# Attention and routed experts on one core: who rounds the keys and queries, how early inputs are fetched, and where the rank products stand

## The chip, the cores and the metric

The kernel runs on one core of a Trainium2 chip. The time is the device time of one launch in microseconds (us); three runs of the kernel before gave 1008.96, 1013.74 and 1014.48, the median is 1013.74. The engines named below are PE (TensorE, matrix products), ACT (ScalarE, activation functions and copies), DVE (VectorE), POOL (GpSimd, which also starts DMAs) and SP (SyncE, which starts most DMAs). Each works through a queue of its own in order, and waits at an instruction until what that needs has been signalled.

## What is computed

```python
# q, k, v: 8 batches x 12 heads x 448 tokens x 64, float32
scores = cap * tanh((q @ k^T / 8) / cap)             # cap = 30
attn   = softmax(scores);  x = attn @ v              # rows of 768 for 3584 tokens
logits = x @ w_gate + modality_bias[modality_id]     # 8 experts
e      = argmax(logits);  gate = softmax(logits)[e]
out    = gate * (relu(x @ w1[e]) @ w2[e])            # 768 -> 1024 -> 768, token's own expert only
```

## The kernel before

Attention works on 48 pairs of heads, `g` = 0 to 47 (six pairs to a batch); an iteration `g` of the loop in `attention` has four steps. The host lays keys (transposed, 512 columns) and queries (448 columns) of a pair side by side in one 128 x 960 tile `kq`. Products in full precision are made of three products of rounded numbers: `hi` is `kq` rounded, `lo` = `kq` - `hi`, and a score is hi·hi + lo·hi + hi·lo (L451). In steps 0 and 2 PE makes the scores of two steps, ACT takes tanh into `th` and exp into `pt` (three tiles) and `sh` (the last 64 keys of both heads). The weighting by values runs one pair behind: in step 1 `weigh_own` (L460) and in step 3 `weigh_shared` (L465) sum into one PSUM tile `xT`, which DVE copies out (L569). That PSUM tile has one buffer, so the next `weigh_own` waits for the copy. DVE also adds the exponentials up in two instructions, `tot` (L548, L549).

Three pairs make a group, and from the fourth pair on each pair also has a share of the work for the group before it. Call them the first, second and third pair (r = 0, 1, 2). The first and second pair's step 1 holds twelve products for sums and logits each (`sums`, L475, PSUM tile `glog`). The second pair's step 3 turns these to token order (`by_token`, tile `lt`) and computes `logits`. The third pair's step 3 is `rows_out`: three sets of four transpositions (L503) into PSUM tiles `tp`, each read by one DVE product into `xs` (L504), which POOL stores. The first and third set share one PSUM buffer, so PE's third set waits for DVE's first `xs`; the second set shares its buffer (tag `small`) with `rank`.

Every sixth pair a batch is complete. `route` then runs a chain of some 15 small DVE instructions to `oh` and `before`, yields, and is taken up again in step 1 of the next pair (a third pair): two small PE products into `rank` (L238, L240), small DVE instructions from there to `pos`, and four POOL DMAs that scatter into `mapd` (L264).

Who makes `hi`: for the first two pairs ACT and DVE; from then on POOL starts a second DMA of `kq` that writes the rounding tile (L436). It may start when PE has read the buffer's old contents; `hi` and `lo` have two buffers. It stands in POOL's queue with the scatters and stores. `prep(g + 1)`, called in step 1 of pair `g`, requests `kq` and `va` (values) over SP's queue; `kq` has two buffers, `va` three.

What sets the order: PE's instructions keep the order of the code (`pin`), and so do SP's loads. DVE's, ACT's and POOL's are put in order by a scheduler when the program is built, which may move an instruction before others of its engine.

At the end, after pair 45, `early_slot` chooses the first expert's rows. SP requests its weights `raw` (four at once), ACT and DVE split them between the last pairs (`SPLITS`, L672 and L673), POOL reads the map (`mt`, L649) and gathers the rows (`xg`, L656), and PE transposes these from step 3 of pair 47 on (`MOVES`, L692). From then on come the expert slots, which the change doesn't touch.

Of the kernel before, what the change touches and what calls it, by code (L numbers as in the profile page):

```python
# [39 lines left out]
F32 = mybir.dt.float32  # L40
# [9 lines left out]
B, H, S, D = 8, 12, 448, 64  # L50
C, CP = 4, 112
NP = H // 2
# [7 lines left out]
VW = 2 * KU * D + 128  # L60
# [15 lines left out]
class Program:  # L76
# [336 lines left out]
    def attention(self, qk, first, rp):  # L413
        tc, nc = self.tc, self.nc
        pe, pin = nc.tensor, self.pin
        with ExitStack() as st:
            ld = st.enter_context(tc.tile_pool(name="ld", bufs=3))
            sp = st.enter_context(tc.tile_pool(name="sp", bufs=2))
            pp = st.enter_context(tc.tile_pool(name="pp", bufs=2))
# [3 lines left out]
            ps_g = st.enter_context(tc.tile_pool(name="ps_g", bufs=1, space=PSUM))  # L423
            ps_v = st.enter_context(tc.tile_pool(name="ps_v", bufs=1, space=PSUM))

            def prep(g):
                b, hp = divmod(g, NP)
                kq = first if g == 0 else self.load_kq(qk, g)
                va = ld.tile([128, VW], F32, name="va")
                self.load(va, self.v[b, hp])  # L430
                hi = sp.tile([128, QK], F32R, name="hi")
                lo = sp.tile([128, QK], F32R, name="lo")
                keep = pin if g < 2 else (lambda inst: inst)

                if g > 1:
                    nc.gpsimd.dma_start(hi, self.kq[b, hp])  # L436
                for cs in (slice(0, QK),) if g else (slice(0, KC2), slice(KC2, QK)):
                    if g < 2:
                        keep((nc.scalar.copy if cs.start else nc.vector.tensor_copy)(hi[:, cs], kq[:, cs]))
                    keep(nc.vector.tensor_tensor(lo[:, cs], kq[:, cs], hi[:, cs], op=ALU.subtract))  # L440
                return hi, lo, va

# [68 lines left out]
            def store(h, xs):  # L511
# [3 lines left out]
                    xs,  # L515
                )

            NG = NP * B

            SPLITS = {  # L520
                (NG - 2, 1): (0,),
                (NG - 2, 3): (1,),
                (NG - 1, 1): (2,),
                (NG - 1, 3): (3,),
                (NG - 0, 0): (4,),
                (NG - 0, 1): (5,),
            }
            MOVES = {(NG - 1, 3): (0, 1), (NG, 1): (2, 3), (NG, 3): (4, 5)}
            self.warm(self.ps_r, 4)
            ready = prep(0)  # L530
            self.gate_weights()
            kept, lgs, routing, raws = {}, {}, {}, []
            for g in range(NG + 1):
                if g < NG:
                    pt = pp.tile([128, 2 * KU, S], F32, name="pt")
                    sh = xp.tile([128, S], F32, name="sh", bufs=HB + 2)
                    cur = ready
                for step in range(C):
                    if step % 2 == 0 and g < NG:
                        scores(step, pt, sh, *cur[:2])  # L540
                        scores(step + 1, pt, sh, *cur[:2])
                    if step == 1:
                        if g + 1 < NG:
                            ready = prep(g + 1)
                        if g:
                            ppt, psh, pva = pend
                            tot = xp.tile([128, 2, S], F32, name="tot", bufs=HB + 1)
                            nc.vector.tensor_tensor(tot, ppt[:, 0:2], ppt[:, 2:4], op=ALU.add)  # L548
                            nc.vector.tensor_tensor(tot, tot, ppt[:, 4:6], op=ALU.add)  # L549
                            xT = ps_x.tile([128, 512], F32, name="xT")  # L550
                            weigh_own(xT, ppt, pva)

                        if g > HB:
                            h, r = divmod(g - HB - 1, HB)
                            if r < 2:
                                sums(h, 2 * r)
                                sums(h, 2 * r + 1)
                        if g in routing:
                            next(routing[g], None)
                            del routing[g]  # L560
                    if step == 3:
                        if g == 3:
                            self.empty_map()
                        if g == 2:
                            self.gate_bias()
                        if g:
                            weigh_shared(xT, psh, pva)
                            xs_ = xp.tile([128, S], F32, name="xT", bufs=HB + 3)
                            nc.vector.tensor_copy(xs_, xT[:, :S])  # L569
                            kept[g - 1] = xs_, tot, psh  # L570
                        if g > HB:
                            h, r = divmod(g - HB - 1, HB)
                            b = h // NH
                            if r == 1:
                                if h % NH == 0:
                                    lgs[b] = xp.tile([CP, C, H, E], F32, name="lg")
                                lt = by_token()
                                rec = logits(h, lt, lgs[b])
                                if h % NH == NH - 1:
                                    way = self.route(b, lgs[b], rp, self.ps_r)  # L580
                                    next(way)
                                    routing[g + 1] = way
                            if r == 2:
                                xs = xp.tile([CP, C, HB * 128], F32, name="xs")
                                for t in range(HB):
                                    rows_out(h, t, xs, rec)
                                store(h, xs)
                                if h == NH * (B - 1) - 1:
                                    meta = self.early_slot(self.cpool, self.ps_r)
                    for k in SPLITS.get((g, step), ()):  # L590
                        self.split_w(raws[k], self.w1s[k], pin=True)
                        if len(raws) < KC:
                            raws.append(self.load_raw(e, self.w1, len(raws), FF))
                    for k in MOVES.get((g, step), ()):
                        self.transpose(k, (ps_s, self.ps_r)[k % 2], ("sc", "small")[k % 2], busy=k < 2)
                if g < NG:
                    pend = pt, sh, cur[2]
                if g == NG - 3:
                    e = self.expert(meta, 0)
                    early = e, self.rows(meta, 0)  # L600
                    raws = [self.load_raw(e, self.w1, k, FF) for k in range(self.nstage)]
                if g == NG - 2:
                    self.gather(early[1], known=NT - S)
# [328 lines left out]
    def build(self):  # L932
        tc, nc = self.tc, self.nc
        with ExitStack() as st:
            self.nstage = 4
            self.cpool = st.enter_context(tc.tile_pool(name="cpool", bufs=1))
            dram = st.enter_context(tc.tile_pool(name="dram", bufs=1, space=DRAM))
            self.plani = self.cpool.tile([1, 3], I32, name="plani")
            with ExitStack() as sa:
                qk = sa.enter_context(tc.tile_pool(name="qk", bufs=2))  # L940
                first = self.load_kq(qk, 0, parts=2)
                with tc.tile_pool(name="ps_w", bufs=1, space=PSUM) as ps_w:
                    self.constants(self.cpool, dram)
                    self.warm(ps_w, 6)
                big = nc.values_load(self.flag[0:1, 0:1], min_val=0, max_val=1)
                with tc.If(big == 0) as branch:
                    with ExitStack() as sb:
                        self.moe_pools(sb)
                        nc.gpsimd.memset(self.xg.bitcast(F32), 0.0)
                        self.ps_r = sb.enter_context(tc.tile_pool(name="ps_r", bufs=1, space=PSUM))  # L950
                        rt = sb.enter_context(tc.tile_pool(name="rt", bufs=1))
                        early, way = self.attention(qk, first, rt)
                        self.moe_pools2(sb)

                        def order():
                            self.meta = self.slots(rt, self.ps_r, True)

                        self.run_slots(early, ((1, lambda: next(way, None)), (3, order)))
                with branch.Else():
                    self.general()  # L960
                    self.tail(fresh=True)
# [70 lines left out]
```

## Time and profile before

| | |
|---|---|
| runs | 1008.96, 1013.74, 1014.48 us |
| profiled execution, its own time | 1010.09 us |
| its span | 1008.5 us |
| PE busy | 926.6 us, 92% |
| ACT busy | 557.2 us, 55% |
| DVE busy | 516.7 us, 51% |
| POOL busy | 157.9 us, 16% |
| granted TensorE clock, mean | 0.965 |
| DMA | 162.63 MB, 161 GB/s |

A group of instructions stands with its busy time, and with the idle time of its engine in front of it and what ended that. PE is busy nearly everywhere from 540 us on, in the expert slots. In the attention part it is busy some 90% of the time: what matters there is which wait ends last in front of PE, and whether the clock is full afterwards.

### The profile page before, as it was taken

Reading aid. Unit: us, or ns where it says so; the run is one execution under the profiler, and the core shown is the slowest. Engines: PE = TensorE matmul, PEld = TensorE weight load, DVE = VectorE, ACT = ScalarE, POOL = GpSimd, SP = SyncE. Lnnn points to the kernel's source line nnn. Section 1 sums busy time; section 2 is a strip of 40 time slices with the busy share of each in tenths; the row PEclk is TensorE's granted clock in tenths of the full one; section 3 lists DMA queues with packets and bytes.
Section 4 is the critical chain, followed back from the end, with each engine's and each line's share of the span. In section 5 each row is a group of like instructions: output and inputs, shape, how many; then the busy total and the mean of one; then the engine's idle time right before and its main releaser. Section 6 shows DMA issues by size and latency. Waiting matters only on the chain. (4 is left out here: it accounts for less than half of the span.)

```text
span 1008.5 us, 14612 instructions
## 1 busy us (share of the span) xinstructions
PE 926.6 (92%) x5360; PEld 709.5 (70%) x5360; DVE 516.7 (51%) x894; ACT 557.2 (55%) x759; POOL 157.9 (16%) x191
## 2 busy tenths in 40 slices
PE   8998998989897998948889999999999999999986
PEld 3444444444454444415889999999999999998886
DVE  4565565646455556727634444443434343428751
ACT  6986777768686778743344444444344344335541
POOL 2003021120212021220242020202020202020000
PEclk9999999999999999969999999999999999999997
DMA  4655646565455546383376363635453635347550
GB/s 137 186 179 120 200 114 193 148 155 177 130 192 126 178 111 215 105 242 98 90 252 225 120 224 121 216 128 190 130 210 129 203 129 190 108 132 259 204 177 5
DMA packets 53803, 162.63 MB, mean 161 GB/s; under 512 B 9422, under 2 KB 9934, under 8 KB 53712
## 3 DMA queue, kind: packets, MB, share of 16 engines
q1 hardware_dynamic: 38000, 105.78, 32.4%
q0 software_dynamic: 15568, 55.72, 19.4%
q8 instruction: 47, 0.77, 0.3%
q14 instruction: 44, 0.36, 0.1%
q10 hardware_dynamic: 144, 0.00, 0.0%
HBM read 139.96 MB, written 22.69 MB: 161 GB/s over the span
## 5 line engine op out<-in xcount | busy, mean ns | idle before, releaser
L453 ACT ACTIVATE th<-sc,isc 128x896 f32<-128x896 f32 x192 | 167.9, 908 | 110.9 <-PE sc L451 110.7
L723 PE MATMUL ph<-x,al 128*128 128x384 f32 (+2 forms) x528 | 168.0, 318 | 0.0
L748 PE MATMUL py<-bh,hh 128*128 128x384 f32 x464 | 159.4, 344 | 3.7 <-ACT hh L729 3.2
L748 PE MATMUL py<-bh,hl 128*128 128x384 f32 x464 | 155.8, 336 | 0.0
L748 PE MATMUL py<-bl,hh 128*128 128x384 f32 x464 | 155.7, 336 | 0.0
L455 ACT ACTIVATE pt<-th,cabs 128x896 f32<-128x896 f32 x144 | 148.0, 1042 | 2.0
L719 PE MATMUL ph<-x,ah 128*128 128x384 f32 x384 | 129.8, 338 | 1.0 <-DVE hl L730 1.0
L460 PE MATMUL xT<-pt,va 128*64 128x448 f32 x576 | 127.8, 582 | 1.9 <-DVE xT L569 1.9
L720 PE MATMUL ph<-x,ah 128*128 128x384 f32 x384 | 129.0, 336 | 0.0
L673 DVE TENSOR_TENSOR bl<-raw,bh 128x768 fp32r<-128x768 f32 x88 | 81.3, 954 | 57.4 <-ACT bh L672 57.1
L440 DVE TENSOR_TENSOR lo<-kq,hi 128x960 fp32r<-128x960 f32 (+2 forms) x49 | 55.6, 1137 | 105.6 <-DMA hi<-in_kq_dram 83.8
L451 PE MATMUL sc<-hi 64*128 64x448 f32 (+1 forms) x336 | 88.4, 453 | 21.5 <-DMA hi<-in_kq_dram 12.9
L672 ACT CAST bh<-raw 128x768 fp32r<-128x768 f32 x88 | 70.2, 839 | 65.3 <-DMA raw<-in_w_dram 57.0
L723 PEld LDWEIGHTS ph<-x,al 128*128 128x128 f32 x528 | 102.7, 194 | 0.0
L451 PEld LDWEIGHTS sc<-hi 64*128 64x128 f32 (+1 forms) x336 | 37.2, 190 | 88.6 <-issue 31.6
L673 DVE TENSOR_TENSOR al<-raw,ah 128x1024 fp32r<-128x1024 f32 x66 | 78.9, 1222 | 32.5 <-ACT ah L672 31.9
L758 POOL DMA_INDIRECT out_dram<-ot,mt x29 | 32.2, 1109 | 388.2 <-ACT ot L753 307.6
L748 PEld LDWEIGHTS py<-bh,hh 128*128 128x128 f32 x464 | 87.4, 188 | 4.8 <-ACT hh L729 3.9
L753 ACT ACTIVATE ot<-py,mt 128x384 f32<-128x384 f32 x58 | 33.6, 580 | 98.4 <-PE py L748 53.9
L460 PEld LDWEIGHTS xT<-pt,va 128*64 128x64 f32 x576 | 39.5, 146 | 68.7 <-issue 54.2
L748 PEld LDWEIGHTS py<-bl,hh 128*128 128x128 f32 x464 | 87.6, 189 | 0.0
L748 PEld LDWEIGHTS py<-bh,hl 128*128 128x128 f32 x464 | 87.5, 189 | 0.1
(160 smaller groups left out, 1332.5 us busy)
## 6 DMA issues: line engine op xcount, KB each, us to landing
raw<-in_w_dram SPq DMA_DIRECT2D x66, 512.0 KB, 4.6
raw<-in_w_dram SPq DMA_DIRECT2D x88, 384.0 KB, 5.1
kq<-in_kq_dram SPq DMA_DIRECT2D x47, 480.0 KB, 3.4
hi<-in_kq_dram POOLq DMA_DIRECT2D x46, 480.0 KB, 4.4
va<-in_v_dram SPq DMA_DIRECT2D x48, 256.0 KB, 4.1
xd<-xs POOLq DMA_DIRECT2D x16, 672.0 KB, 4.4
mapd<-pay,pos POOLq DMA_INDIRECT x32, 4.6
xg<-xd,mt POOLq DMA_INDIRECT x30, 6.0
```

The lines of the kernel that those rows point to most:

```text
L440: keep(nc.vector.tensor_tensor(lo[:, cs], kq[:, cs], hi[:, cs], op=ALU.subtract))
L451: pin(pe.matmul(sc[:, j, :S], k[rows, ks], q[rows, KC2:], start=i == 0, stop=i == 2))
L453: nc.scalar.activation(th[:, :n], sc[:, :n, :S], AF.Tanh, scale=self.isc)
L455: nc.scalar.activation(dst, th[:, :n] if step < KU else th[:, 0], AF.Exp, scale=self.cabs)
L460: pin(pe.matmul(xT[j * D : (j + 1) * D, :S], va[:, u * D : (u + 1) * D], pt[:, u], start=u < 2, stop=False))
L672: a = self.nc.scalar.copy(hi, raw)
L673: b = self.nc.vector.tensor_tensor(lo, raw, hi, op=ALU.subtract)
L719: nc.tensor.matmul(ph[:, :w], hi[:, fs], self.x[:, k, 0, :w], start=first, stop=False)
L720: nc.tensor.matmul(ph[:, :w], hi[:, fs], self.x[:, k, 1, :w], start=False, stop=False)
L723: nc.tensor.matmul(ph[:, :w], lo[:, fs], self.x[:, k, 0, :w], start=False, stop=last)
L748: nc.tensor.matmul(py[:, :HALF], self.h[a][:, f, rows], self.w2s[f][c][:, cs], start=i == 0, stop=i == 3 * FC - 1,)
L753: nc.scalar.mul(ot[:, cs], py[:, :HALF], mt[:, t, 1:2])
```

## The change

`hi` is made by DVE for all pairs (line 441 of the changed kernel), by a cast from `kq`, as for pair 1 before; POOL's DMA for it goes. The requests of `kq` and `va` leave `prep` for a function `fetch`, called once for pairs 0 and 1 at the start and then for pair `g + 2` in step 3 of pair `g`; `kq` gets a third buffer. The second half of `route` is taken up in step 3 of its pair, before `weigh_shared`, instead of in step 1 behind `weigh_own`.

```diff
+            def fetch(g):
+                if g < NG:
+                    kq = first if g == 0 else self.load_kq(qk, g)
+                    va = ld.tile([128, VW], F32, name="va")
+                    self.load(va, self.v[g // NP, g % NP])
+                    fetched[g] = kq, va
             def prep(g):
-                kq = first if g == 0 else self.load_kq(qk, g)
-                va = ld.tile([128, VW], F32, name="va")
-                self.load(va, self.v[b, hp])
+                kq, va = fetched.pop(g)
...
-                if g > 1:
-                    nc.gpsimd.dma_start(hi, self.kq[b, hp])
                 for cs in (slice(0, QK),) if g else (slice(0, KC2), slice(KC2, QK)):
-                    if g < 2:
-                        keep((nc.scalar.copy if cs.start else nc.vector.tensor_copy)(hi[:, cs], kq[:, cs]))
+                    keep((nc.scalar.copy if cs.start else nc.vector.tensor_copy)(hi[:, cs], kq[:, cs]))
                     keep(nc.vector.tensor_tensor(lo[:, cs], kq[:, cs], hi[:, cs], op=ALU.subtract))
...
+            fetch(0)
             ready = prep(0)
             self.gate_weights()
+            fetch(1)
...
-                        if g in routing:
-                            next(routing[g], None)
-                            del routing[g]
                     if step == 3:
+                        if g in routing:
+                            next(routing.pop(g), None)
...
+                        fetch(g + 2)
...
-                qk = sa.enter_context(tc.tile_pool(name="qk", bufs=2))
+                qk = sa.enter_context(tc.tile_pool(name="qk", bufs=3))
```

The scheduler gives DVE another order. DVE before, around a third pair without a batch's end (the numbers tell tiles of one name apart; `lo_1699` is for the pair after next, counted from the one in whose step 3 `xT_1625` is copied):

```order
L548 TENSOR_TENSOR tot_1702<-pt_1592 128x896
L569 COPY xT_1650<-xT_1625 128x448
L504 TENSOR_TENSOR xs_1652<-tp_1653,rec_1588 112x4x128
L504 TENSOR_TENSOR xs_1652<-tp_1659,rec_1588 112x4x128
L549 TENSOR_TENSOR tot_1702<-tot_1702,pt_1592 128x896
L504 TENSOR_TENSOR xs_1652<-tp_1665,rec_1588 112x4x128
L440 TENSOR_TENSOR lo_1699<-kq_1694,hi_1698 128x960
```

DVE now, at the same place:

```order
L552 TENSOR_TENSOR tot_1702<-pt_1596 128x896
L441 CAST hi_1698<-kq_1652 128x960
L442 TENSOR_TENSOR lo_1699<-kq_1652,hi_1698 128x960
L572 COPY xT_1650<-xT_1625 128x448
L506 TENSOR_TENSOR xs_1656<-tp_1657,rec_1592 112x4x128
L506 TENSOR_TENSOR xs_1656<-tp_1663,rec_1592 112x4x128
L553 TENSOR_TENSOR tot_1702<-tot_1702,pt_1596 128x896
L506 TENSOR_TENSOR xs_1656<-tp_1669,rec_1592 112x4x128
```

The new cast and the subtraction stand between the first `tot` and the copy of `xT`; before, the subtraction stood behind all three `xs`. They stand in front of the copy in the other pairs too.

DVE now, around a third pair in which a batch is routed:

```order
L552 TENSOR_TENSOR tot_1974<-pt_1840 128x896
L234 TENSOR_TENSOR acc_115<-before_1834,oh_1832 112x8
L259 TENSOR_REDUCE gs_1905<-ex_1826 112x4
L260 TENSOR_SCALAR gs_1905<-gs_1905 112x4
L441 CAST hi_1970<-kq_1924 128x960
L244 TENSOR_TENSOR rows_1896<-rank_1893,region_103 112x32
L261 RECIPROCAL pay_1903<-gs_1905 112x4
L442 TENSOR_TENSOR lo_1971<-kq_1924,hi_1970 128x960
L247 TENSOR_TENSOR rows_1896<-rows_1896,oh_1832 112x32
L572 COPY xT_1922<-xT_1869 128x448
L249 TENSOR_REDUCE posf_1899<-rows_1896 112x4
L506 TENSOR_TENSOR xs_1928<-tp_1929,rec_1816 112x4x128
```

Before, the small instructions from `rank` to `pos` all stood ahead of that copy, and cast and subtraction were not among them; now they are spread between these.

POOL before, over one batch (`hi` is the DMA that goes):

```order
L436 DMA hi_2856<-in_kq_dram 128x960
L264 DMA mapd_71<-pay_2880,pos_2878 31104x2 x4
L436 DMA hi_2964<-in_kq_dram 128x960
L255 IOTA pay_3377 112x4
L513 DMA xd_70<-xs_2918 448x1x384
L436 DMA hi_3031<-in_kq_dram 128x960
```

POOL now, over the same batch:

```order
L515 DMA xd_70<-xs_2650 448x1x384
L264 DMA mapd_71<-pay_2897,pos_2895 31104x2 x4
L515 DMA xd_70<-xs_2922 448x1x384
L255 IOTA pay_3394 112x4
L515 DMA xd_70<-xs_3147 448x1x384
```

What waited behind the scatters for its turn, `hi` of the pairs that follow, is no longer in this queue.

## Rows read from the trace of the kernel before

**Rows 1.** Page: PE's busy time, granted clock in 40 slices of the span
```profile
PE 926.6 (92%) x5360; PEld 709.5 (70%) x5360; DVE 516.7 (51%) x894; ACT 557.2 (55%) x759; POOL 157.9 (16%) x191
...
PEclk9999999999999999969999999999999999999997
```
**Rows 2.** Waits of PE: line, what ended them, us in total, times, longest
```profile
PE sc L451 <- DMA hi<-in_kq_dram: 12.9, 6, 3.1
PE sc L451 <- DVE lo L440: 11.0, 8, 6.7
PE rank L238 <- DVE oh L228: 10.9, 7, 1.8
PE sc L451 <- ACT th L453: 7.6, 2, 7.3
PE tp L503 <- DVE xs L504: 7.0, 14, 1.1
```
**Rows 3.** Timeline, start and length: exponentials of pairs 5 and 45; score starts
```profile
53.93 0.67 ACT L455 ACTIVATE sh<-th,cabs 128x448 f32<-128x448 f32 x1
...
223.22 0.47 PE L451 MATMUL sc<-hi 64*128 64x448 f32 x2
...
231.37 0.47 PE L451 MATMUL sc<-hi 64*128 64x448 f32 x2
...
247.36 0.47 PE L451 MATMUL sc<-hi 64*128 64x448 f32 x2
...
423.67 0.66 ACT L455 ACTIVATE sh<-th,cabs 128x448 f32<-128x448 f32 x1
```
**Rows 4.** Timeline of DVE and PE in a third pair, then a first
```profile
228.50 1.09 DVE L548 TENSOR_TENSOR tot<-pt 128x896 f32<-128x896 f32 x1 [0.78 <-ACT pt L455]
...
229.52 0.62 DVE L569 COPY xT<-xT 128x448 f32<-128x448 f32 x1
...
230.05 1.28 DVE L504 TENSOR_TENSOR xs<-tp,rec 112x512 f32<-112x512 f32 x2
...
230.79 0.65 PE L503 MATMUL tp<-ident,xT 128*112 128x128 f32 x4 [0.44 <-DVE xs L504]
...
238.17 0.36 PE L451 MATMUL sc<-lo,hi 128*128 128x448 f32 x1
...
240.63 0.60 PE L460 MATMUL xT<-pt,va 128*64 128x448 f32 x2
```
**Rows 5.** Timeline at the start: DVE's two casts, POOL's fill
```profile
5.49 2.02 POOL L949 MEMSET xg<- 128x2304 f32 x1 [2.32 <-DVE identr L108]
...
5.81 1.98 DVE L439 CAST hi<-kq 128x512 fp32r<-128x512 f32 x1 [0.45 <-issue]
...
11.10 0.66 DVE L439 CAST hi<-kq 128x960 fp32r<-128x960 f32 x1 [1.99 <-DMA kq<-in_kq_dram]
```
**Rows 6.** Timeline of DVE: a late subtraction, what follows it, the rank's reader
```profile
212.30 1.16 DVE L440 TENSOR_TENSOR lo<-kq,hi 128x960 fp32r<-128x960 f32 x1 [8.51 <-DMA hi<-in_kq_dram]
...
213.38 1.08 DVE L548 TENSOR_TENSOR tot<-pt 128x896 f32<-128x896 f32 x1
...
421.23 0.18 DVE L244 TENSOR_TENSOR rows<-rank,region 112x32 f32<-112x32 f32 x1
```
**Rows 7.** Windows: length, busy (count) PE PEld DVE ACT POOL, clock, DMA, GB/s
```profile
85.00:90.00 5.00, 4.65 (x21) 3.16 (x19) 2.82 (x14) 3.13 (x4) 2.62 (x3) 0.67 0.43 6
...
250.00:255.00 5.00, 3.35 (x20) 1.77 (x17) 4.66 (x21) 3.54 (x5) 0.00 (x0) 1.00 0.31 106
...
325.00:330.00 5.00, 4.07 (x18) 1.89 (x20) 3.69 (x4) 2.82 (x4) 0.00 (x0) 0.72 0.91 290
```
**Rows 8.** Timeline near the end of attention
```profile
447.48 0.74 PE L451 MATMUL sc<-hi,lo 64*128 64x448 f32 x2 [6.73 <-DVE lo L440]
...
448.24 1.07 POOL L656 DMA_INDIRECT xg<-xd,mt  x1 [8.40 <-DMA mt<-mapd]
...
458.14 0.43 PE L692 MATMUL ptr<-identr,xg 128*128 128x128 f32 x3
```

More of the change, by code (lines that the diff above doesn't have):

```diff
@@ L416, in attention @@
         with ExitStack() as st:
+            NG = NP * B
             ld = st.enter_context(tc.tile_pool(name="ld", bufs=3))
@@ L424, in attention @@
             ps_v = st.enter_context(tc.tile_pool(name="ps_v", bufs=1, space=PSUM))
+            def fetch(g):
[4 more added lines that the diff above has]
+                    fetched[g] = kq, va
             def prep(g):
-                b, hp = divmod(g, NP)
-                kq = first if g == 0 else self.load_kq(qk, g)
-                va = ld.tile([128, VW], F32, name="va")
-                self.load(va, self.v[b, hp])
+                kq, va = fetched.pop(g)
                 hi = sp.tile([128, QK], F32R, name="hi")
@@ L516, in store @@
                 )
-            NG = NP * B
             SPLITS = {
@@ L529, in attention @@
             self.warm(self.ps_r, 4)
+            fetched = {}
+            fetch(0)
             ready = prep(0)
             self.gate_weights()
+            fetch(1)
             kept, lgs, routing, raws = {}, {}, {}, []
@@ L557, in attention @@
                                 sums(h, 2 * r + 1)
+                    if step == 3:
                         if g in routing:
-                            next(routing[g], None)
-                            del routing[g]
-                    if step == 3:
+                            next(routing.pop(g), None)
                         if g == 3:
```

## The prediction

> **What bounds the kernel now.** First the page: PE is busy 92% of the span [rows 1], so time goes only where PE waits or runs at a lower clock; in the 40 slices the clock is nearly everywhere full, with a dip in the slice near 450 us. Then the waits of PE [rows 2]: those on `hi`, `lo`, `oh` and the second `xs` lie in attention. Then the timeline, for what a pair costs when nothing is late: from one third pair to the next, score start to score start, 24.14 us for three pairs (223.22 to 247.36 [rows 3]), in which ACT and DVE have room. From the exponentials of pair 5 to those of pair 45 it takes 423.67 - 53.93 = 369.7 us [rows 3]. These 40 pairs would take 13.33 × 24.14 = 321.9 us without hindrance; so 47.8 us are there to be had or lost. I read them as: 12.9 us on `hi`, 4.3 us on `lo` (11.0 less the longest, 6.7, which is in the end part), 10.9 us on `oh` [rows 2], and the clock. The windows of 5 us show where it falls to the lower of its two levels, 1.2 GHz: a row at 0.67 [rows 7] has lost 5 × 0.33 = 1.65 us of full speed if PE had work. Between pairs 5 and 45 there are eight such rows below 0.8 (first and last in [rows 7]) and a ninth dip split over two; nine make about 15 us. 28.1 + 15 = 43 of the 47.8 are named; some 5 us remain as late consequences.
>
> **The DMA that goes.** 46 DMAs of 480 KB leave POOL's queue. Their delay behind the scatters is what makes `lo` start at 212.30, after 8.5 us of idle DVE [rows 6]; with it go 12.9 + 4.3 = 17.2 us of PE's waits. What is late next is DVE's queue, below. `kq` was already in the box in time except now and then; asked for a pair earlier it lands well ahead of its cast, so a third buffer and the earlier request cost nothing and take nothing from PE by themselves. On SP the request of `va` waits until `weigh_shared` has freed a buffer, and the next `kq` is queued behind it; that is still about a pair ahead of the cast that needs it. At the start one more `kq` and `va` share the DMA engines with those of pair 1; a microsecond at most, taken as 0.
>
> **The cast.** Alone it took 0.66 us for 960 columns; a cast of 512 columns took 1.98 us while POOL filled a tile, from 5.49 to 7.51 [rows 5]. Those are the bounds; in pairs POOL computes next to nothing, so 0.66. The Trainium skill says (SBUF — State Buffer, Who interferes with whom) that such a copy and a GpSimd instruction share a port pair, which one takes wholly, so that the other waits until it has finished. The trace agrees: 1.98 us beside POOL's fill, 0.66 alone; by that rule a cast that met POOL would cost up to the length of POOL's instruction, and the sum with it stands under the rivals.
>
> **Where the cast stands.** This decides. DVE takes it and the subtraction before the copy of `xT`, and so before the first `xs`, for which PE's third set of transpositions waits. In a third pair [rows 4]: `tot` starts at 228.50, its successor 1.02 us later; before, that was the copy (229.52), then `xs` (230.05) and PE's third set at 230.79, after 0.44 us of waiting. Now cast and subtraction come between: 0.70 us from the cast's start to the subtraction's (0.66 and a signal), 1.08 from the subtraction to its successor (212.30 to 213.38 [rows 6]), together 1.78 us. The cast has no other wait: PE has read the old `hi` by then. So the third set starts at 232.57, PE waits 2.2 us instead of 0.44, and every third pair grows by 1.78 us. 13 of them lie between pairs 5 and 45: 23.1 us.
>
> In a first pair the cast waits for PE's last score product (238.17 + 0.36, with a signal 238.6 [rows 4]); subtraction 239.3, copy 240.4 to 241.0. `weigh_own` stood ready at 240.63 and needs the copy: 0.43 us, 13 times 5.6 us. In a second pair the same reckoning leaves 0.08 us, 1.0 us in all.
>
> **The rank products.** Seven times PE waited for `oh`, 10.9 us [rows 2], 1.6 us each. Behind four score steps instead of two, about 1.5 us later, most of this is covered; I leave 0.5 us each. But now the small instructions behind `rank` mix with cast and copy: some four of 0.18 us [rows 6] stand ahead of the first `xs`, 0.7 us more of the same wait. 7 × 1.2 = 8.4 us. Bounds: 0, if all of it hides; 7 × 2.3 = 16 us, if the old wait stays and the 0.7 comes on top. The scatters start some 3 us later and nobody is behind them but the stores.
>
> **The clock.** Of 13 waits on `oh` (7) and `hi` (6), nine were followed by a dip. A stretch like 250 to 255, with 1.65 us idle, kept 1.00 [rows 7]. The new waits of 2.2 us stand between the two kinds. With the same share, 13 × 9/13 = 9 dips × 1.65 = 14.9 us; bounds 0 and 14 × 1.65 = 23.
>
> **The end.** From 432 us on PE waited 7.3 us for ACT, which waited for the first `raw`, and 6.7 us for `lo` of pair 47 [rows 2, 8], whose `kq` had been requested behind four `raw`. The second goes: `kq` is requested in pair 45 ahead of them. The first stays. But the gather was started at 448.24, after 8.4 us of waiting for `mt`, and PE's transpositions of its rows at 458.14 waited for nothing [rows 8]; its chain starts with the scatters, which come later. So between 0 and 6.7 us are saved; I take 5, as the stores and loads in front of `mt` thin out.
>
> **Sum.** 321.9 + 23.1 + 5.6 + 1.0 + 8.4 + 14.9 = 374.9 us for pairs 5 to 45, against 369.7: +5.2. The end -5. Together +0.2 on 1010.09 us, the profiled execution's own time, which is 3.65 below the median of the runs; on the median 1013.74 + 0.2 = 1014 us. PE's wait moves from a DMA behind POOL's scatters to DVE's queue. Its own range is 1009 to 1019.
>
> **Rivals.** (a) The clock holds through waits of 2.2 us: 14.9 us less, 999 us. For it: the 1.65 us that cost nothing [rows 7]. Against: most waits of about 2 us did cost.
> (b) It drops after every wait of a third pair, and from about the twelfth dip on the kernel is slower by over 0.5%. 14 dips instead of 9 are 8.2 us, and their consequences, in the proportion of the 5 us unnamed above, another 3: 1025 us. For it: the wait is longer than those on `oh` (1.6 us), four of which dipped out of seven. Against: 250 to 255.
> (c) Casts are out of the way after all, for instance because `tot` starts earlier when PE is late: the 29.7 us of the two terms for third and first pairs vanish, and the dips (14.9) with them; with the end's 5 that is 374.9 - 29.7 - 14.9 - 5 against 369.7, or 969 us. For it: DVE is idle for 49% of the span [rows 1]. Against: a queue in order doesn't care for shares.
> (d) Casts meet POOL's scatters or stores and take 1.98 us: 1.3 us more on each of the 13 third pairs, 17 us, 1031 us. Against: the scatters end before the next pair's cast.
>
> **Chances.** Forecast 0.38, (a) 0.22, (b) 0.27, (c) 0.08, (d) 0.05. What a measurement of this kernel can tell from no change is about 0.5%, 5 us. Faster: (a) and (c), 0.30; slower: (b) and (d), 0.32; the same 0.38. The range reaches from (a) to (b) with a little beyond each, 998 to 1027, and leaves out (c) and (d).
>
> **What would show it.** In the profile after: PE's waits on `hi` and on `lo` gone; `tp` waiting for `xs` some 2.2 us in each of 14 third pairs, about 30 us in all, where it was 7.0; `rank` waiting 0.5 us or less; `xT` waiting for its copy in first pairs; casts of 0.66 us. Rows of the clock below 0.8 count the dips: nine confirm, none or fourteen are (a) or (b). Waits of `tp` under 0.6 us would make the main step wrong.

## The result and the profile after

The changed kernel took 1006.12 us in the median of 20 executions (994.81 to 1015.57), the kernel before 1011.15 us beside it on the same chip (1007.53 to 1017.61): ratio 0.9919, 95% interval 0.9894 to 0.9945. The ratio leaves out the five executions of the changed kernel at the lowest granted clock (0.954 to 0.959), which the median holds; the medians as they stand give 0.9950. On a second chip it was 1004.28 against 1016.11 us, ratio 0.9898 (0.9856 to 0.9940). So the change makes the kernel 0.5 to 1% faster, where "no change" was forecast; the time lies in the range given.

The profiled execution took 1000.30 us of its own time, span 998.6 us; before it was 1010.09 and 1008.5. The first lies 5.8 us under the median of its kernel, the second 1.1 us, so this pair of profiles shows a larger change than the medians do. The page, beside [rows 1]:

```profile
PE 923.6 (92%) x5360; PEld 709.6 (71%) x5360; DVE 542.2 (54%) x940; ACT 555.5 (56%) x759; POOL 132.6 (13%) x145
...
PEclk9999999999899999988999999999999999999998
```

DVE gained 46 instructions and 25.5 us, POOL lost 46 and 25.3 us. PE's waits (what ended them: us in total, times, longest), beside [rows 2]:

```profile
PE tp L505 <- DVE xs L506: 28.2, 15, 2.2
PE ptr L696 <- DMA xg<-xd,mt: 11.5, 5, 4.6
PE xT L462 <- DVE xT L572: 6.5, 17, 1.6
PE sc L453 <- ACT th L455: 6.1, 3, 5.2
PE tp L505 <- DVE rows L244: 4.1, 7, 0.6
```

The waits on `hi`, `lo` and `oh` are gone; in their place stand `tp` on `xs` with 28.2 us (before 7.0), `xT` on its copy, and at the end `ptr` on the gathered rows with 11.5 us (before 3.1). The timeline of one third pair, the answer to [rows 4]:

```profile
225.27 1.09 DVE L552 TENSOR_TENSOR tot<-pt 128x896 f32<-128x896 f32 x1 [2.38 <-ACT pt L457]
...
226.28 0.65 DVE L441 CAST hi<-kq 128x960 fp32r<-128x960 f32 x1
...
226.97 1.16 DVE L442 TENSOR_TENSOR lo<-kq,hi 128x960 fp32r<-128x960 f32 x1
...
228.04 0.62 DVE L572 COPY xT<-xT 128x448 f32<-128x448 f32 x1
228.57 1.28 DVE L506 TENSOR_TENSOR xs<-tp,rec 112x512 f32<-112x512 f32 x2
...
229.31 0.65 PE L505 MATMUL tp<-ident,xT 128*112 128x128 f32 x4 [2.15 <-DVE xs L506]
```

That is the step that the forecast called decisive, and it is as forecast: cast and subtraction push the copy from 1.02 us behind the start of `tot` to 2.77 us, and PE's third set waits 2.15 us instead of 0.44 us.

Where the time went shows in three stretches: pairs 5 to 45 (exponentials to exponentials, as in [rows 3]), then to the first expert product, then to the end of the span. The windows give PE, PEld, DVE, ACT and POOL busy, then the granted clock, the DMA engines' share and GB/s. Before:

```profile
53.93:423.67 369.74, 333.75 (x1940) 168.39 (x1936) 214.29 (x387) 275.54 (x328) 63.45 (x83) 0.96 0.56 158
423.67:472.26 48.59, 30.16 (x173) 14.25 (x172) 25.35 (x42) 22.12 (x28) 10.31 (x12) 0.82 0.58 170
472.26:1008.50 536.24, 514.10 (x3016) 503.75 (x3013) 248.00 (x418) 218.00 (x355) 75.84 (x72) 0.98 0.49 162
```

After:

```profile
55.71:421.63 365.92, 330.68 (x1936) 167.87 (x1932) 234.73 (x422) 273.60 (x328) 39.76 (x43) 0.96 0.34 108
421.63:469.16 47.53, 32.12 (x175) 15.29 (x175) 26.31 (x50) 21.81 (x28) 12.34 (x11) 0.86 0.55 153
469.16:998.63 529.47, 511.92 (x3016) 503.16 (x3013) 248.03 (x418) 218.45 (x355) 75.73 (x72) 0.99 0.50 164
```

The start is 1.8 us longer (pair 5 at 55.71, not 53.93; 1.6 of it lie between the exponentials of pair 0 and those of pair 5), the pairs 3.8 us shorter, the end 1.1 us shorter, the expert part 6.8 us shorter though its instructions are the same: together -9.9 us. Of the 6.8, 2.9 us lie behind the last product. The last row of each profile, before and then after:

```profile
999.65 0.98 POOL L758 DMA_INDIRECT out_dram<-ot,mt  x1 [25.79 <-POOLq L811]
```

```profile
992.64 0.98 POOL L762 DMA_INDIRECT out_dram<-ot,mt  x1 [23.73 <-POOLq L815]
```

From the end of that row to the end of the span it is 7.9 us before and 5.0 after; the trace shows POOL draining its queue there, 7.64 and 4.76 us long. Of the other 3.9 us, up to the last product, some 1.7 are clock: ahead of that product the trace has the low level (1.2 GHz) for 10.2 us before and 6.8 us after. Another 1.7 are PE's waits, many small ones that sum to 12.4 us before and 10.7 after.

### The profile page after: what moved, and what is told of

The parts are those of the page before. It is cut to its first block, busy times and chain, and to the rows that moved or that the text cites. A ratio compares the mean times of both kernels' runs of the same rounds, so it can differ in the third digit from the quotient of the medians.

```text
span 998.6 us, 14505 instructions
## 1 busy us (share of the span) xinstructions
PE 923.6 (92%) x5360; PEld 709.6 (71%) x5360; DVE 542.2 (54%) x940; ACT 555.5 (56%) x759; POOL 132.6 (13%) x145
## 5 line engine op out<-in xcount | busy, mean ns | idle before, releaser
L552 DVE TENSOR_TENSOR tot<-pt 128x896 f32<-128x896 f32 x48 | 52.4, 1091 | 122.3 <-ACT pt L457 68.9
L453 PE MATMUL sc<-hi 64*128 64x448 f32 (+1 forms) x336 | 90.7, 469 | 6.7 <-ACT th L455 6.1
L677 DVE TENSOR_TENSOR al<-raw,ah 128x1024 fp32r<-128x1024 f32 x66 | 78.8, 1222 | 28.7 <-ACT ah L676 28.2
L676 ACT CAST ah<-raw 128x1024 fp32r<-128x1024 f32 x66 | 66.6, 1048 | 33.4 <-DMA raw<-in_w_dram 31.8
```

What stands on the lines that cost most here:

```text
L453: pin(pe.matmul(sc[:, j, :S], k[rows, ks], q[rows, KC2:], start=i == 0, stop=i == 2))
L676: a = self.nc.scalar.copy(hi, raw)
L677: b = self.nc.vector.tensor_tensor(lo, raw, hi, op=ALU.subtract)
```

## The experiments

The working theory after the result: each edit acts by itself, and the cast's place on DVE gives back most of what the others win. The rivals: the place doesn't matter; only the clock's luck differs. The first row is that of the result. In the order of the paragraphs below, the first four kernels ran beside each other on one chip (before: 1016.64 us) and the next four on another (1016.11), but for a single run among these; that run and the last three belong to a third set (1016.44). "Clock" is the median of the granted clock over the executions; for the kernel before it was 0.962 or 0.963 in these three sets. The last column is that of the one profiled execution.

| kernel | median us | ratio, 95% interval | clock | pairs 5 to 45 |
|---|---|---|---|---|
| changed | 1006.12 | 0.9919 (0.9894 to 0.9945) | 0.966 | 365.9 |
| changed, again | 1004.28 | 0.9898 (0.9856 to 0.9940) | 0.968 | 367.5 |
| rank move alone | 1010.60 | 0.9950 (0.9923 to 0.9978) | 0.968 | 370.6 |
| cast alone | 999.07 | 0.9859 (0.9824 to 0.9893) | 0.974 | 363.3 |
| early fetch alone | 1018.67 | 1.0033 (1.0011 to 1.0055) | 0.962 | 378.1 |
| cast and early fetch | 992.02 | 0.9787 (0.9748 to 0.9827) | 0.979 | 365.0 |
| changed, last rank in old place | 1003.67 | 0.9853 (0.9805 to 0.9901) | 0.965 | 371.4 |
| changed, cast twice | 983.54 | 0.9676 (0.9636 to 0.9715) | 0.983 | 351.5 |
| changed, cast last | 971.02 | 0.9580 (0.9542 to 0.9617) | 0.976 | 334.6 |
| cast last, ranks in old place | 966.88 | 0.9505 (0.9476 to 0.9535) | 0.982 | 331.7 |
| the same, weights later | 965.17 | 0.9508 (0.9471 to 0.9545) | 0.981 | 331.7 |

The edits do not act by themselves: alone they give -0.5% (rank move), -1.4% (cast) and +0.3% (early fetch), cast and early fetch together -2.1%, and all three -0.8 to -1.0%.

**Rank move alone.**

```
-                        if g in routing:
-                            next(routing[g], None)
-                            del routing[g]
                     if step == 3:
+                        if g in routing:
+                            next(routing.pop(g), None)
```

> The kernel before with one edit, the rank products at the end of a pair; keys and queries still fetched twice, by SP and by POOL. Theory (each edit acts by itself, and the cast's place on VectorE gives back most of what the others win): PE's wait of rank on oh, 10.9 us in seven batches, goes; about 1 us per batch comes back as small VectorE instructions ahead of the first xs; the waits on hi (12.9 us) stay. With two to four dips of the clock fewer: 1011 - 10.9 + 7 - 4 = about 1003 us. Rival 1 (the rank products only gain where the cast is on VectorE too, since hi is fetched behind the scatters, which now come later): the waits on hi grow by what oh gives, 1011 us or more. Rival 2 (the whole gain of 5 us is the clock's luck): 1011 us with the wait on oh gone and nothing in its place.

The lines move from step 1 to step 3. 1010.60 us, ratio 0.9950: neither the theory's 1003 nor the first rival's loss. The wait on `oh` goes as the theory has it, but the profile shows another in its place, and none on `hi` any more:

```profile
PE lt L484 <- DVE gl L481: 23.9, 6, 5.0
```

`lo` waits for `hi`, fetched behind the scatters, and `gl` stands behind `lo` on DVE. So the first rival had the mechanism (the wait on the DMA grows and moves; 23.9 us is about what the waits on `hi` and `oh` were together), without its price: the pairs of this profile took 370.6 us, as much as in the first profile before, in an execution 4.6 us over the median.

**Cast alone.**

```
-                if g > 1:
-                    nc.gpsimd.dma_start(hi, self.kq[b, hp])
                 for cs in ...
-                    if g < 2:
-                        keep(...copy(hi[:, cs], kq[:, cs]))
+                    keep(...copy(hi[:, cs], kq[:, cs]))
```

> The kernel before with one edit, VectorE's cast of the upper halves in place of POOL's DMA; the inputs are fetched one pair ahead with two buffers, the rank products stand where they stood. Theory (the cast's place on VectorE, ahead of the copy of xT and the first xs, costs more than the DMA did): waits on hi and lo go, 17.2 us; waits of tp on xs rise from 7 to about 28 us and of xT on its copy from under 1 to about 6 us; the wait on oh stays: 1011 + 27 - 17 - up to 5 at the end = about 1016 to 1021 us. Rival (VectorE is idle for nearly half of the span, so its queue costs nothing): 1011 - 17 = 994 us.

999.07 us: the theory's sum missed. It had the kernel 5 to 10 us slower than before; beside the 1016.64 us of this chip it is some 14 to 18 us faster. The rival's 17 us came out, but not for its reason: DVE's queue does cost (waits of `tp` on `xs` 22.5 us in all, of `xT` 7.1), and yet the kernel is faster, so the DMA had cost more than its 17 us of waits. The drain at the end is the short one already here, so it goes with POOL's 46 DMAs.

**Cast and early fetch, ranks in their old place.** The changed kernel with the edit of the first experiment taken back.

> The changed kernel with the rank products back in their old place; cast and earlier fetch stay. Theory (each edit acts by itself): the wait on oh comes back, 10.9 us less about 1 us per batch that the move had cost at the first xs, with one to three dips: 1006 + 4 + 3 = about 1011 to 1016 us; waits of tp about 27 us as in the changed kernel. Rival (the cast is what gains and the rank products do nothing): 1006 us.

992.02 us: both missed. The rank move, which looked like the harmless part, loses 1.1 to 1.3% of the time once the cast is on DVE. The early fetch, which loses alone, gains beside the cast (0.9859 to 0.9787): with the cast alone PE waited 11.8 us for the `hi` of pair 47, here not, and from pair 45's exponentials to the first expert product it takes 40.3 us instead of 49.5. PE's waits:

```profile
PE tp L505 <- DVE xs L506: 21.8, 15, 2.1
PE rank L238 <- DVE oh L228: 8.8, 7, 1.3
```

From the starts of `sh`, the two intervals around a batch's end took 8.52 + 10.80 us without a dip of the clock, and 6.97 + 11.99 us in the changed kernel. So the wait on `oh` costs 0.36 us per batch more, not 1.3: PE waits less for `xs` when it has waited for `oh` already. But dips (stretches at the low level) cost 0.5 to 1.1 us in the first of these intervals here and almost nothing in the second; in the two profiles of the changed kernel they cost 1.3 to 2.9 us in the second. In the profiles the pairs differ by 0.9 us only and the way from there to the first expert product by 7.2. The rest of the 12 to 14 us, some 4 to 6, is what the profiled executions of the changed kernel lie under their medians; where it is lost no profile shows.

**Cast last.** The same instructions as the changed kernel; on DVE the code's order is kept for cast, subtraction, the copy of `xT` and `xs`.

```
-                keep = pin if g < 2 else (lambda inst: inst)
+                keep = pin
...
-                            nc.vector.tensor_copy(xs_, xT[:, :S])
+                            pin(nc.vector.tensor_copy(xs_, xT[:, :S]))
...
-                nc.vector.tensor_tensor(xs[...], ...)
+                pin(nc.vector.tensor_tensor(xs[...], ...))
```

> The changed kernel with the order on VectorE fixed: in each pair the copy of xT and the three xs come ahead of the next pair's cast and subtraction; the same instructions, nothing added. Theory (what the cast costs is its place ahead of them): waits of tp on xs fall from 28 us to about 5, of xT on its copy from 6.5 to under 1, and most of the seven dips between pairs 5 and 45 go: 1006 - 23 - 6 - 4 to 9 = 968 to 973 us; the time from the exponentials of pair 5 to those of pair 45 falls from 365.9 to about 332 us. Rival (PE waits there for something else, and the cast only hides it): no wait goes, 1000 to 1006 us. A second rival: cast and subtraction are now late for the next pair's scores, so that sc waits for lo about 1 us in each pair: 1010 us or more.

971.02 us, pairs 5 to 45 in 334.6 us: the theory holds, with its size; neither rival does. DVE and PE in a third pair:

```profile
210.76 1.09 DVE L552 TENSOR_TENSOR tot<-pt 128x896 f32<-128x896 f32 x1 [0.32 <-ACT pt L457]
...
211.77 0.62 DVE L572 COPY xT<-xT 128x448 f32<-128x448 f32 x1
212.31 1.28 DVE L506 TENSOR_TENSOR xs<-tp,rec 112x512 f32<-112x512 f32 x2
...
213.04 0.65 PE L505 MATMUL tp<-ident,xT 128*112 128x128 f32 x4 [0.44 <-DVE xs L506]
...
215.10 0.65 DVE L441 CAST hi<-kq 128x960 fp32r<-128x960 f32 x1
```

The cast comes behind the last `xs`, PE's wait is the 0.44 us of [rows 4], and the clock of these pairs is 0.99:

```profile
53.44:388.03 334.59, 319.41 (x1936) 162.14 (x1932) 234.46 (x420) 273.16 (x329) 51.40 (x43) 0.99 0.40 118
```

**The changed kernel again**, on the chip of the next three.

> The changed kernel itself, beside the next three on one chip. So far the cast and earlier fetch without the rank move came out at 0.9787 of the kernel before, the whole change at 0.9919 on another chip: the rank move, forecast as 8.4 us of new cost against 10.9 us of an old wait, seems to lose 13 us. Theory (real: 7 us at the end, where PE waits for the gathered rows, and the rest lower clock): ratio 0.990 to 0.994, granted clock about 0.966 in the median. Rival (the chip made the difference): 0.979 here, clock about 0.978.

Ratio 0.9898, clock 0.968, as on the first chip: the rival is out, the loss with the rank move stands. Cast and early fetch without it ran on one chip alone, a third.

**The last batch's rank products in their old place.** The condition becomes `step == (1 if g == NG - HB else 3)`.

> The changed kernel with the rank products of the last of the seven batches, the one whose scatters the gather waits for, back in the old place; the other six stay at the end of their pairs. Theory (the move loses at the end because the scatters, the table read and the gather come about 5 us later): PE's wait of ptr on the gathered rows falls from 11.5 to about 5 us, the time from the exponentials of pair 47 to the first expert product from 19.6 to about 13.4 us, ratio lower by 0.006 than the changed kernel beside it; the waits of tp stay at 28 us. Rival (the gather waits for something else, such as raw's loads): ptr's wait stays, no difference.

From pair 47's exponentials to the first expert product it takes 13.4 us instead of 19.6, as the theory has it; PE's wait on the gathered rows:

```profile
PE ptr L696 <- DMA xg<-xd,mt: 4.5, 4, 1.7
```

POOL at the end, in this kernel (first scatter, read of the map, first gather):

```profile
425.46 0.99 POOL L264 DMA_INDIRECT mapd<-pay,pos  x1 [22.30 <-DVE pos L251]
...
439.26 0.60 POOL L653 DMA_DIRECT2D mt<-mapd  x1 [0.64 <-issue]
447.83 1.07 POOL L660 DMA_INDIRECT xg<-xd,mt  x1 [7.97 <-DMA mt<-mapd]
```

and in the changed kernel:

```profile
425.14 0.99 POOL L264 DMA_INDIRECT mapd<-pay,pos  x1 [26.38 <-DVE xs L506]
...
440.03 0.61 POOL L653 DMA_DIRECT2D mt<-mapd  x1 [9.16 <-DMA mapd<-pay,pos]
...
446.69 3.41 POOL L660 DMA_INDIRECT xg<-xd,mt  x1 [5.89 <-issue]
```

Pair 45's exponentials start at 426.99 us here and at 421.63 there: counted from them the scatters begin 5 us earlier here (-1.5, not +3.5), and the gather 4.2 us earlier. The ratio to the kernel before fell from 0.9898 to 0.9853, less than the 0.006 expected, with intervals that overlap; the medians as they stand, 0.9884 and 0.9878, hardly differ. So the wait is shown by the profile, its gain not by the times: the pairs of this profile took 371.4 us, with 37.5 us at the low level. What the move costs beyond the end must by difference (0.9787 without it, on another chip) be in the other six batches.

**Cast last, all ranks in their old place.**

> The cast-last kernel with all seven rank products in their old place. With cast and subtraction behind the xs, the rank move had no tp wait left to avoid. Theory (the rank move costs at the end and gains only PE's wait on oh): ptr's wait falls by about 6 us, the wait of rank on oh comes back with about 9 to 11 us, of which the 7.7 us of tp on rows go: within 5 us of the cast-last kernel, ratio 0.950 to 0.960. Rival (the rank move spoils the clock whatever VectorE's order is): ratio 0.945, clock 0.98 or more.

966.88 us, 0.9505, at the theory's lower edge, but not by its terms: the wait on `oh` came back with 2.5 us, not 9 to 11, and ptr's wait didn't fall (11.3 us, 11.4 with the cast last alone). Of the rival the clock came (0.982; between pairs 5 and 45 of the profile it is 1.00), the ratio of 0.945 not. So the move loses with this order on DVE too, 0.7% (0.9580 against 0.9505). The scatters begin 1.3 us behind pair 45's exponentials, where they begin 1.4 us ahead of them with cast and early fetch, and POOL then waits 10.9 us for them to land, not 5.8.

**The same kernel, one more profile.**

> The cast-last kernel with the old rank place once more, one look, beside the next ones on one chip. Expected as before: ratio 0.948 to 0.954, about 967 us; pairs 5 to 45 in about 332 us; waits of ptr 8 to 12 us.

968.01 us, pairs 5 to 45 in 331.7 us, as expected; ptr's wait, 12.9 us, is a little over the 8 to 12 expected.

**Early fetch alone.** The third buffer, `fetch` and its calls put into the kernel before; POOL's DMA stays.

> The kernel before with one edit, the inputs of SP fetched two pairs ahead with a third buffer; the upper halves still come by POOL's DMA, the rank products stand where they stood. Theory (SP's kq was in time but at the end): only the wait of sc on lo of pair 47, 6.7 us, goes, so 0 to 7 us less, ratio 0.993 to 1.000; waits on hi stay at about 13 us. Rival (the earlier loads crowd POOL's DMA out): waits on hi grow, ratio 1.005 or more.

1018.67 us, 0.3% slower: neither the theory's 0.993 to 1.000 nor the rival's 1.005. The long wait on `lo` of pair 47 goes, but:

```profile
PE sc L457 <- DMA hi<-in_kq_dram: 19.4, 7, 5.5
```

This looks like the rival's wait. But 4.1 us of it are a wait at pair 46, which the first profile before does not have; the six waits between pairs 5 and 45 sum to 15.3 us, and what they are without the early fetch needs the next run.

**The kernel before, one more profile.**

> The kernel before, one more profile. In the first one pairs 5 to 45 took 369.7 us and its span times its granted clock was 973, near the low end of what runs of it gave later (972.5 to 981.6, median 977). Theory (its waits on hi and oh vary from run to run): pairs 5 to 45 take 370 to 378 us here, with waits on hi between 13 and 20 us. Rival (the attention part is the same in every run, and only the clock moves): 369 to 371 us with about nine dips.

1019.03 us; pairs 5 to 45 took 378.9 us, just above the theory's range, with the waits on `hi` inside it:

```profile
PE sc L451 <- DMA hi<-in_kq_dram: 19.0, 6, 4.8
PE rank L238 <- DVE oh L228: 11.3, 7, 1.9
PE sc L451 <- DVE lo L440: 9.7, 7, 6.5
```

So the kernel before has 12.9 us on `hi` in one execution and 19.0 in another, and the early fetch's 15.3 lie between: that it crowds the DMA out does not show. New with the early fetch alone are 3.7 us of `lt` on `gl`, and 12.6 us on `oh` instead of 10.9 and 11.3; whether these are its 0.3% one profile doesn't tell. In six intervals of the pairs behind a batch's end, where `hi` is waited for, the first profile before lost 27.5 us against the undisturbed 7.88 us each, the second 39.4 us: waits, dips and all. Which is the usual two profiles don't tell: the first execution lay 1.1 us under the median beside it, the second 2.6 us over.

**Weights a pair later**, on the best kernel so far: the four `raw` are requested after pair 46 instead of 45, and the splits follow one to two pairs later.

> The cast-last kernel with the old rank place; the first four loads of expert weights are requested one pair later, and their splits stand one to two pairs later, so that ScalarE no longer waits for them ahead of pair 46's tanh. Theory (these loads, 512 KB each, hold up the landing of the scatters and ScalarE): POOL's wait of mt on the scatters falls from 10.9 to about 6 us, PE's wait on ScalarE (6 us) goes, ptr's wait falls below 6 us: 966.9 - 5 to 10 = 957 to 962 us, ratio 0.941 to 0.946. Rival (the weights then arrive late for the first expert product): PE waits 5 to 10 us for al or ah, 967 to 972 us.

965.17 us, 0.9508: no change; theory and rival both missed. ACT's wait goes, and PE then waits 16.5 us on the gather instead of 11.3. POOL still waits 10.5 us for the scatters to land, so the weights don't hold them up. What does wasn't found.

**Cast twice.** The changed kernel, with one more line:

```
                     keep((nc.scalar.copy if cs.start else nc.vector.tensor_copy)(hi[:, cs], kq[:, cs]))
+                    if g > 1:
+                        nc.vector.tensor_copy(hi[:, cs], kq[:, cs])
```

> The changed kernel with each cast of pairs 2 to 47 done twice, the same values. VectorE does 46 casts more, 30 us of work; but the subtraction now stands behind the copy of xT and, in third pairs, behind the first xs, so that ahead of them stand two casts (about 1.36 us) and not a cast and a subtraction (1.78 us). Theory (the place on VectorE counts, not the amount of work): third pairs shrink by 0.4 us, the waits of tp fall from 28 to about 22 us, xT's waits from 6.5 to under 3, with up to three dips fewer: 1005 - 8 to 13 = 992 to 997 us, ratio 0.977 to 0.983. Rival (VectorE's work as such costs): ratio above the changed kernel's 0.990, 1006 to 1030 us.

983.54 us, 2% less than the changed kernel, with 46 casts of 0.66 us more on DVE (busy 567.1 us, not 542.2). A third pair:

```profile
223.03 0.66 DVE L441 CAST hi<-kq 128x960 fp32r<-128x960 f32 x1 [0.63 <-PE sc L455]
223.73 0.66 DVE L443 CAST hi<-kq 128x960 fp32r<-128x960 f32 x1
224.31 0.62 DVE L574 COPY xT<-xT 128x448 f32<-128x448 f32 x1
224.84 1.28 DVE L508 TENSOR_TENSOR xs<-tp,rec 112x512 f32<-112x512 f32 x2
...
225.57 0.65 PE L507 MATMUL tp<-ident,xT 128*112 128x128 f32 x4 [0.95 <-DVE xs L508]
226.03 1.15 DVE L444 TENSOR_TENSOR lo<-kq,hi 128x960 fp32r<-128x960 f32 x1
```

The scheduler now puts the subtraction behind the first two `xs`; PE waits 0.95 us, not 2.15. Such third pairs shrink by 0.5 to 0.8 us, where 0.4 was expected. The gain is about twice what was expected, and most of the surplus is the clock: between pairs 5 and 45 it is at the low level for 10.2 us, in the changed kernel for 27.3. Not all went as expected: `xT` waits 10.3 us for its copy, not under 3, and `rank` 9.0 us for `before`. What the run shows is that more work on DVE, placed otherwise, took less time; so the amount of work is not what costs.

## Why the prediction was wrong

The sum of the prediction for pairs 5 to 45, term by term, against the first pair of profiles (from the 48 starts of `sh`; 13 third and 13 first pairs):

| term | forecast | measured |
|---|---|---|
| undisturbed pairs | 321.9 | 320.4 |
| third pairs | +23.1 | 13 x 1.76 = +22.9 |
| first pairs | +5.6 | 13 x 0.38 = +4.9 |
| second pairs | +1.0 | 0 |
| rank products | +8.4 | 7 x 0.12 + 6 x 0.84 = +5.9 |
| clock | +14.9 | +11.8 |
| sum | 374.9 | 365.9 |

The intervals of one third pair, before and then after, 9.39 and 11.15 us from `sh` to `sh`:

```profile
230.72 0.66 ACT L455 ACTIVATE sh<-th,cabs 128x448 f32<-128x448 f32 x1
...
240.11 0.66 ACT L455 ACTIVATE sh<-th,cabs 128x448 f32<-128x448 f32 x1
```

```profile
227.48 0.66 ACT L457 ACTIVATE sh<-th,cabs 128x448 f32<-128x448 f32 x1
...
238.63 0.66 ACT L457 ACTIVATE sh<-th,cabs 128x448 f32<-128x448 f32 x1
```

- **The step that failed: the sizes in the sum.** No mechanism in the pairs failed, and no term is far off, but all miss to the same side, by 9.0 us in all. The clock (14.9 us forecast, 11.8 measured) and the rank products (8.4 and 5.9) are 5.6 of it. 1.5 are a slip for the most part: 40 pairs are 13 times three and one more, and that one is a short interval of 6.85 us, where 13.33 times 24.14 takes 8.05. The other 1.9 are in the second, first and third pairs. What was put at nothing is the other part: outside the pairs -5 us were forecast, all at the end, and -6.1 came (+1.8, -1.1, -6.8), with 6.8 in the expert part, 2.9 of them POOL's shorter drain. Together these are the 10.1 us between the forecast's +0.2 and the -9.9 of the first pair of profiles. Up to half of that miss can be the draw of the two profiled executions: the medians differ by 5.0 us on that chip, though by 11.8 on the second.
- **Where the cast stands: right**, mechanism and size. Cast-last, same instructions in another order, takes the 2.15 us to 0.44, and shows what the place cost with all that follows: 31 us of the 366. Rival (c), which had 969 us for a cast out of the way, is what that kernel does: 971. (Its 29.7 us are those of third, first and second pairs; third and first alone are 28.7.)
- **The casts' 0.66 us: right.** In the changed kernel (duration ns: minimum, median, maximum):

```profile
L441 DVE CAST hi<-kq x48: 652/660/2126, 5.8 to 421.0; 128x960 fp32r<-128x960 f32 x47, 128x512 fp32r<-128x512 f32 x1
```

  The one long cast is that of 512 columns at the start, beside POOL's fill; rival (d) didn't happen. In the pairs of this profile one cast met POOL for more than 0.02 us:

```profile
210.81 0.66 DVE L441 CAST hi<-kq 128x960 fp32r<-128x960 f32 x1 [0.47 <-PE sc L453]
211.06 0.45 POOL L255 IOTA pay<- 112x4 int32 x1 [2.54 <-DMA mapd<-pay,pos]
```

  The cast went first and kept its 0.66 us; POOL's instruction, 0.12 to 0.16 us in the other batches, took 0.45 us and ended 0.04 us behind the cast. The rule of the Trainium skill (SBUF — State Buffer, Who interferes with whom), that one of the two takes the shared port pair and the other waits until it has finished, agrees with these two rows. In the other kernels casts ran beside scatters and stores of POOL, and took 0.65 to 0.92 us. With the cast alone one took 0.66 us wholly inside a scatter (200.15 us; the scatter from 199.93 to 200.93), so it did not wait for the end of that, and (d)'s 1.98 us do not come there either.
- **The DMA that goes: priced too low, but not in the sum.** 17.2 us were the waits of one profile. In that profile the six intervals in which `hi` is waited for lost 27.5 us, in the next 39.4. The 374.9 us do not use this price, as they start from undisturbed pairs; it is part of the 369.7 us that they were set against, and that base is as uncertain as the miss is large. Against the second profile's 378.9 the same 374.9 would have read -4, and the changed kernel's second profile has -11.4 (378.9 to 367.5). Where the price did mislead is the cast alone, expected 5 to 10 us slower and found faster.
- **The rank products: 8.4 us in the forecast, 5.9 measured.** Without dips the balance with the old wait is nearly nothing, as the forecast had it, since the old wait hides behind the new one. Not seen was that the move makes one long wait of two short ones, and that dips then cost more in the intervals where it stands. Cast and early fetch without the move run at a clock of 0.979, with it at 0.966 to 0.968. That the longer wait is the reason for the whole of this fits the intervals, but is not shown.
- **The clock: nine dips forecast, 14.9 us.** Both profiles have seven between pairs 5 and 45, some longer than others, 27.3 and 30.7 us at the low level, at a cost of 11.8 and 13.4 us: the size was near. The shorter ones cost 1.3 to 1.6 us each, not 1.65. The clock goes with the wait of the third pairs, as the forecast had it: where that is 0.95 us the low level lasts 10.2 us, where it is 0.44 us 6.8 or none. Rivals (a) and (b), no dips or fourteen, are both out.
- **The end: 5 us forecast, 1.1 measured.** The wait on `lo` of pair 47 went, and the later scatters ate it, by the rank move: 6.2 us, as the last-rank run shows. They started 3.5 us behind pair 45's exponentials, 0.7 us ahead of them before, and what is behind them here is not only stores but the gather.
- **The early request: forecast to cost nothing.** Alone it lost 0.3%, a loss not traced; beside the cast it gained, at the end.
- **The start and the expert part: 0 forecast.** The 1.8 us at the start were not traced to a cause. In the expert part the drain, 2.9 us, is real. The other 3.9 us go with the clock: up to the last product that part took 520.3 to 523.1 us in the six profiles that have the low level for 13.7 us or less in it, and 523.4 to 527.1 us in the eight with 17.1 us or more, whichever kernel. Why the clock differs there stays open.

## What to carry to other kernels

A stall behind a queue's DMAs can vary from run to run (12.9 and 19.0 us here): before a change is weighed against it, take a second profile, and price it by the length of the intervals in which it stands, dips included, and not by the wait's row. When work moves to an engine with time to spare, ask what it is put in front of: here the place of two instructions on DVE was worth 3%, and two casts with the subtraction behind cost less than one cast with the subtraction in front. A sum of many small terms can be right in each and wrong in its sign, when the change is smaller than what they miss together. Two waits on one path don't add; taking the first away can leave one long wait where two short ones were.

## What was not expected of the hardware

POOL's drain behind the last store took 7.63 to 7.64 us in all four profiles whose POOL had started the 46 DMAs of `hi` (191 POOL instructions in all), the last of them some 570 us earlier, and 4.76 to 4.78 us in the ten without (145). The granted clock, more than the sum of waits, separates two kernels that do the same work: changed, and cast with early fetch, differ by 0.9 us in the pairs of their profiles, by 12 to 14 us in the median time and by 0.011 to 0.013 in the median clock. The span times the granted clock, in the median of the executions, is 970.2 us for the one and 968.6 for the other. With the last rank in its old place it is 966.2 at a clock of 0.965: there the wait at the end is gone, and the clock stays where it was.
